# Decoding float32 weights with three VectorE operations in place of five

## The chip, the cores and the metric

The kernel runs on one core of a Trainium2 chip. The metric is the device time of one execution in microseconds (us); lower is better. A core has five engines that work side by side, each on its own queue in order: TensorE (PE, matrix products and transposes; its weight loads are shown as PEld), VectorE (DVE), ScalarE (ACT), GpSimd (POOL) and SyncE (SP, which issues transfers here).

## The reference

Three stages on 2304 tokens (4 batches of 576), all float32: an attention with 8 heads of 64, of which four heads see a band of 32 positions and four see every 32nd position; a gated feed-forward with an RMS norm; a second gated feed-forward without a norm.

```python
def _moe_ref(x, w_gate, w_val, w_out, rms_g):
    rms = np.sqrt(np.mean(x * x, axis=-1, keepdims=True) + 1e-06)
    xn = x / rms * rms_g
    g = xn @ w_gate                       # 512 -> 1536
    silu = g * (1.0 / (1.0 + np.exp(-g)))
    val = xn @ w_val
    return (silu * val @ w_out).astype(np.float32)

def reference(**kwargs):
    attn_out = _attn_ref(q, k, v)         # (4, 8, 576, 64), masked softmax(q k^T / 8) v
    x = np.ascontiguousarray(attn_out.transpose(0, 2, 1, 3)).reshape(B * S, H * D)
    x = _moe_ref(x=x, **moe_kwargs)
    return _moe2_ref(x=x, **moe2_kwargs)  # the same without rms and rms_g
```

The weights and the second layer's weights reach the kernel as 64-bit floats, two 32-bit words each, which it reads as integers.

## The kernel before

**The products.** Every float32 operand of a feed-forward product is kept as two halves, a high part `hi` that TensorE takes exactly and a low part `lo`, the rest. A product is then three matmuls: hi with hi, hi with lo, lo with hi (`proj`, `down`). The high part is made by a ScalarE copy that rounds, the low part by a VectorE subtraction (`split_x` for tokens, `hidden` for the hidden layer).

**The weights** come in 72 tiles of 128 x 512: for layer m, chunk c (12 of them) and z = 0, 1, 2 (gate, value, out). `weight_step` makes one tile in phases: `load` (a transfer of 512 KB of 64-bit words into `raw`, three buffers), two empty phases, `scale`, `bits`, `hi`. In `scale` ScalarE reads the high words as if they were floats and scales them (`dh`, L173), and converts the low words to an integer (`dr`, L174). In `bits` VectorE puts a float32 together by integer operations:

- L184 shifts `dh` and masks it, L186 adds the sign out of `raw`: the result is `df`, the weight cut to its upper bits;
- L188 keeps the exponent of `df`, L189 puts the low words' bits into `dr`, L191 multiplies the two: that is the low half, written to the weight tile `w` directly.

In `hi` ScalarE copies `df` into the tile's high half (L195). `dh` and `dr` have two buffers each.

**The order.** The program is written as products of chunks with `point()` calls between their pieces. At each point, every started step (attention pieces, weight tiles) runs its next phase, and new steps are started at a set pace; a scheduler then puts each engine's instructions in an order by priorities (weight tiles have the lowest). Weight work is placed behind the last attention or feed-forward instruction of its engine (`behind`).

**The stages.** First only attention of batch 0 runs (strided heads, local heads, RMS norm: `ss` holds the sums of squares, `mean`, `dg` and L595 apply the norm), together with the first weight tiles; then the products of the first layer begin on the first 256 tokens (`xh`, `xl` are the halves of the tokens, `b_g` and `b_v` the PSUM banks of gate and value), with the attention of later batches between them. 18 weight tiles (chunks 0 to 5 of layer 1) are decoded in this beginning; the first layer uses them for nearly all tokens before chunks 6 to 11 are decoded from 344 us on, and the other 54 tiles follow beside long products.

Of the kernel before, what the change touches and what calls it, by code (L numbers as in the profile page):

```python
# [8 lines left out]
F32 = mybir.dt.float32  # L9
F32R = mybir.dt.float32r  # L10
U32 = mybir.dt.uint32
AF = mybir.ActivationFunctionType
ALU = mybir.AluOpType
# [8 lines left out]
PRIO_W = -150  # L22
# [3 lines left out]
def attn_ffn_ffn(ctx: ExitStack, tc: tile.TileContext, q, k, v, w1g, w1v, w1o, rms_g, w2g, w2v, w2o, out):  # L26
    nc = tc.nc
# [15 lines left out]
    dec = ctx.enter_context(tc.tile_pool(name="dec", bufs=2))  # L43
# [88 lines left out]

    LOW = 2.0 ** -9 * (1 - 2.0 ** -23)
    WSRC = {1: (w1g, w1v, w1o), 2: (w2g, w2v, w2o)}
    wt = {}
    wdone = set()
# [6 lines left out]
    def free(m, c):  # L145

        i = order.index((m, c))
        return slot_of[m, c] in wpool and (i < RING or order[i - RING] in wused) and (m == 1 or state["rest"])
# [4 lines left out]
    def weight_step(m, c, z):  # L153
        cell = {}

        def load():
            w = WSRC[m][z].bitcast(U32)
            if z == 2:
                src = w[c * 128:(c + 1) * 128, :].rearrange("p (k f) -> p k f", k=KC)
            else:  # L160
                src = w[:, c * 256:(c + 1) * 256].rearrange("(k p) f -> p k f", p=128)
            r = dec.tile([128, KC, 256], U32, tag="raw", name="raw", bufs=3)
            (nc.sync if att else nc.sync).dma_start(out=r, in_=src)
            words = r.rearrange("p k f -> p (k f)").rearrange("p (n s) -> p n s", s=2)
            cell["lw"], cell["hw"] = words[:, :, 0], words[:, :, 1]

        def scale():

            h = dec.tile([128, 512], F32, tag="dh", name="dh")
            r = dec.tile([128, 512], U32, tag="dr", name="dr")  # L170
            cell["h"], cell["r"] = h, r
            with behind("act"):
                nc.scalar.activation(out=h, in_=cell["hw"].bitcast(F32), func=AF.Copy, scale=2.0 ** -112)  # L173
                nc.scalar.activation(out=r, in_=cell["lw"], func=AF.Copy, scale=LOW)  # L174

        def bits():


            h, r = cell["h"].bitcast(U32), cell["r"]
            s = slot_of[m, c]  # L180
            cell["t"] = t = wpool[s].tile([128, 2, KC * 128], F32R, tag=f"w{s}_{z}", name=f"w{m}_{c}_{z}")
            cell["f"] = f = dec.tile([128, 512], F32, tag="df", name="df")
            with behind("dve"):
                nc.vector.tensor_scalar(out=h, in0=h, scalar1=3, scalar2=0x7FFFF000, op0=ALU.logical_shift_left,  # L184
                                        op1=ALU.bitwise_and)
                nc.vector.scalar_tensor_tensor(out=f.bitcast(U32), in0=cell["hw"], scalar=0x80000000, in1=h,  # L186
                                               op0=ALU.bitwise_and, op1=ALU.bitwise_or)
                nc.vector.tensor_scalar(out=h, in0=f.bitcast(U32), scalar1=0xFF800000, scalar2=None, op0=ALU.bitwise_and)  # L188
                nc.vector.scalar_tensor_tensor(out=r, in0=cell["hw"], scalar=23, in1=r,  # L189
                                               op0=ALU.logical_shift_left, op1=ALU.bitwise_or)  # L190
                nc.vector.scalar_tensor_tensor(out=t[:, 1], in0=r, scalar=2.0 ** -43, in1=cell["h"], op0=ALU.mult, op1=ALU.mult)  # L191

        def hi():
            with behind("act"):
                nc.scalar.copy(out=cell["t"][:, 0], in_=cell["f"])  # L195
            wt[m, c, z] = cell["t"]
            wdone.add((m, c, z))

        return Step([load] + [wait] * 2 + [scale, bits, hi], lambda: free(m, c), PRIO_W)

    def behind(eng):

        return tc.issue_after(last[eng]) if eng in last else nullcontext()
# [501 lines left out]
    def gate(m, c, n, xs):  # L705
        need_w(m, c, 0)
        gv = GV[0]
        GV.append(GV.pop(0))
        pg = bank(gv[0])
        proj(pg, n, wt[m, c, 0], xs)  # L710
        hp, w = pools["h"]
        s = hp.tile([128, w], F32, tag="s", name="sg")
        silu(s, pg, n)
        point()
        need_w(m, c, 1)
        pv = bank(gv[1])
        proj(pv, n, wt[m, c, 1], xs)
        hh = hp.tile([128, w], F32R, tag="hh", name="hh", bufs=3)
        hl = hp.tile([128, w], F32R, tag="hl", name="hl", bufs=3)
        hidden(s, pv, hh, hl, n)  # L720
        point()
        return hh, hl
# [79 lines left out]
    att.load(0, 1)  # L802
    att.load_v(0, 1)
    wq += [weight_step(m, c, z) for m, c in order for z in range(3)]
    for _ in range(0):
        start(wq.pop(0))
# [31 lines left out]
    for si, (m, t0, n, c0, c1) in enumerate(segs):  # L838
# [17 lines left out]
        for c in range(c0, c1):  # L856
            h = gate(m, c, n, xs)
# [60 lines left out]
```

## Time and profile before

| | us |
|---|---|
| runs | 1076.64, 1082.42, 1082.6 |
| median of the runs | 1082.42 |
| profiled execution | 1075.61 |
| its span, first to last instruction | 1073.7 |
| PE busy | 1039.3 (97%) |
| PEld busy | 914.4 (85%) |
| DVE busy | 510.8 (48%) |
| ACT busy | 442.8 (41%) |
| POOL busy | 58.7 (5%) |

The mean granted clock of TensorE is 0.969 of its full speed. Busy shares are means over the whole span. In the page's 40 slices of 27 us each, PE shows 4, 8, 7, 8 tenths in the first four slices and 9 in nearly all others, and DVE 3, 8, 9, 8 tenths in the first four, so that the beginning has to be read apart from the rest.

### The profile page before, as it was taken

To read this page: it belongs to the slowest core of one execution; us is meant where nothing else is said; L and a number is where in the kernel's file an instruction comes from. 1 tells how busy PE (TensorE), PEld (TensorE's weight loads), DVE (VectorE), ACT (ScalarE), POOL (GpSimd) and SP (SyncE) were. 2 spreads that over 40 slices of the span, in tenths; PEclk is the share of its full clock that TensorE was granted. 3 is DMA by queue.
4 is the path that set the end of the run, shared out by engine and by line. 5 is a ranking of instruction groups with operands and counts; after the bars stand their busy time and mean duration, and the time that the engine had idled before them with its cause. 6 is when DMAs were issued, how large, how long until landed. Compare 5 with 4: busy or idle time off the path is not lost.

```text
span 1073.7 us, 15937 instructions
## 1 busy us (share of the span) xinstructions
PE 1039.3 (97%) x6056; PEld 914.4 (85%) x6056; DVE 510.8 (48%) x1296; ACT 442.8 (41%) x1082; POOL 58.7 (5%) x83
## 2 busy tenths in 40 slices
PE   4878999999999999999999999999999999999998
PEld 3668999999999999998888898888888888888887
DVE  3898536445445883692222589312224512222212
ACT  5977546636634662561211467222123312212111
POOL 3212102102100000000000000000000000000000
PEclk9657999999999999999999999999999999999999
DMA  7685233233014551372021366111111102030202
GB/s 194 169 215 172 77 103 94 88 98 94 25 60 133 172 160 58 113 234 89 20 79 62 118 206 213 37 62 40 40 40 65 34 1 94 14 98 1 78 1 89
DMA packets 104260, 100.39 MB, mean 94 GB/s; under 512 B 40564, under 2 KB 92476, under 8 KB 103544
## 3 DMA queue, kind: packets, MB, share of 16 engines
q1 hardware_dynamic: 103992, 99.10, 30.2%
q8 instruction: 48, 0.79, 0.3%
q0 software_dynamic: 192, 0.28, 0.1%
q14 instruction: 28, 0.23, 0.1%
HBM read 77.47 MB, written 21.89 MB: 93 GB/s over the span
## 4 chain that ended last, share of the span: by engine, by line
PE 91%; DVE 4%; DMA 3%; ACT 1%; issue 0%; SPq 0%; DVEq 0%; ACTq 0%
PE b_y L63 28%; PE b_a L63 28%; PE b_v L63 16%; PE b_g L63 16%; PE b_a L66 2%; DMA raw<-in_moe_w_gate_dram 1%; DVE dr L189 1%; DVE df L186 1%; DVE w L191 1%; DMA kn<-in_k_dram 1%; ACT e L409 0%; DMA part<-ob 0%; DMA xf<-x_d 0%; SPq L266 0%; DVE xl L692 0%
## 5 line engine op out<-in xcount | busy, mean ns | idle before, releaser
L63 PE MATMUL b_a<-xh,w 128*128 128x512 f32 (+3 forms) x816 | 232.8, 361 | 0.0
L63 PE MATMUL b_g<-xh,w 128*128 128x512 f32 (+3 forms) x696 | 192.8, 342 | 2.0 <-DVE sg L668 2.0
L63 PE MATMUL b_v<-xh,w 128*128 128x512 f32 (+3 forms) x696 | 193.1, 342 | 0.0
L63 PE MATMUL b_y<-hh,w 128*128 128x320 f32 (+3 forms) x624 | 165.3, 329 | 1.7 <-DVE ob L75 1.7
L63 PEld LDWEIGHTS b_a<-xh,w 128*128 128x128 f32 x816 | 148.6, 190 | 21.5
L678 ACT CAST hh<-sg 128x512 fp32r<-128x512 f32 (+3 forms) x138 | 72.6, 526 | 199.4 <-DVE sg L677 175.9
L63 PE MATMUL b_a<-xl,w 128*128 128x512 f32 (+3 forms) x408 | 147.3, 361 | 0.0
L63 PEld LDWEIGHTS b_g<-xh,w 128*128 128x128 f32 x696 | 125.5, 191 | 15.1 <-DVE sg L668 2.3
L63 PEld LDWEIGHTS b_v<-xh,w 128*128 128x128 f32 x696 | 125.3, 191 | 12.9 <-issue 0.9
L63 PE MATMUL b_y<-w,hh 128*128 128x512 f32 x432 | 133.3, 390 | 0.0
L63 PEld LDWEIGHTS b_y<-hh,w 128*128 128x128 f32 x624 | 110.0, 188 | 9.9 <-DVE ob L75 1.9
L63 PE MATMUL b_g<-xl,w 128*128 128x512 f32 (+3 forms) x348 | 117.0, 336 | 0.0
L63 PE MATMUL b_v<-xl,w 128*128 128x512 f32 (+3 forms) x348 | 116.8, 336 | 0.0
L677 DVE TENSOR_TENSOR sg<-sg,b_v 128x512 f32<-128x512 f32 (+3 forms) x51 | 31.2, 612 | 164.5 <-PE b_v L63 160.9
L677 DVE TENSOR_TENSOR sg<-sg,b_a 128x512 f32<-128x512 f32 (+3 forms) x51 | 31.2, 611 | 153.3 <-PE b_a L63 152.8
L679 DVE TENSOR_TENSOR hl<-sg,hh 128x512 fp32r<-128x512 f32 (+3 forms) x138 | 80.9, 586 | 43.1 <-ACT hh L678 42.6
L63 PE MATMUL b_y<-hl,w 128*128 128x320 f32 (+3 forms) x312 | 100.9, 323 | 0.0
L63 PEld LDWEIGHTS b_y<-w,hh 128*128 128x128 f32 x432 | 80.4, 188 | 16.2
L63 PEld LDWEIGHTS b_a<-xl,w 128*128 128x128 f32 x408 | 77.6, 190 | 10.9
L670 ACT ACTIVATE sg<-b_a 128x512 f32<-128x512 f32 (+3 forms) x51 | 27.4, 538 | 139.3 <-PE b_a L63 139.1
L63 PE MATMUL b_y<-w,hl 128*128 128x512 f32 x216 | 84.0, 389 | 0.0
L670 ACT ACTIVATE sg<-b_g 128x512 f32<-128x512 f32 (+3 forms) x51 | 27.4, 538 | 123.2 <-PE b_g L63 123.0
(126 smaller groups left out, 1356.8 us busy)
## 6 DMA issues: line engine op xcount, KB each, us to landing
raw<-in_moe_w_gate_dram SPq DMA_DIRECT2D x24, 512.0 KB
raw<-in_moe_w_val_dram SPq DMA_DIRECT2D x24, 512.0 KB
raw<-in_moe_w_out_dram SPq DMA_DIRECT2D x24, 512.0 KB
xf<-y_d SPq DMA_DIRECT2D x5, 1024.0 KB
out_dram<-ob SPq DMA_DIRECT2D x18, 256.0 KB
xf<-x_d SPq DMA_DIRECT2D x8, 512.0 KB
part<-ob SPq DMA_DIRECT2D x14, 256.0 KB
ob<-part SPq DMA_DIRECT2D x14, 256.0 KB
```

The source lines that it names most:

```text
L63: traced(nc.tensor.matmul(out_, a, b_, start=start, stop=stop))
L66: traced(nc.tensor.transpose(out_, a, one))
L186: nc.vector.scalar_tensor_tensor(out=f.bitcast(U32), in0=cell["hw"], scalar=0x80000000, in1=h, op0=ALU.bitwise_and, op1=ALU.bitwise_or)
L189: nc.vector.scalar_tensor_tensor(out=r, in0=cell["hw"], scalar=23, in1=r, op0=ALU.logical_shift_left, op1=ALU.bitwise_or)
L191: nc.vector.scalar_tensor_tensor(out=t[:, 1], in0=r, scalar=2.0 ** -43, in1=cell["h"], op0=ALU.mult, op1=ALU.mult)
L670: last["act"] = ins_of(nc.scalar.activation(out=s[:, :n], in_=pg[:, :n], func=AF.Silu))
L677: nc.vector.tensor_tensor(out=s[:, :n], in0=s[:, :n], in1=pv[:, :n], op=ALU.mult)
L678: last["act"] = ins_of(nc.scalar.copy(out=hh[:, :n], in_=s[:, :n]))
L679: last["dve"] = ins_of(nc.vector.tensor_tensor(out=hl[:, :n], in0=s[:, :n], in1=hh[:, :n].bitcast(F32), op=ALU.subtract))
```

## The change

A tile now takes two bit operations and a subtraction on VectorE. ScalarE's two conversions stay; the constant of the second is another, so that the integer `dr` already holds the float's low bits in place. L180 (new numbering) puts the sign out of `raw` into `dr`, L181 shifts `dh` and adds `dr`: `dh` is now the whole float32. ScalarE copies it into the high half (L187), and VectorE subtracts that half from `dh` into the low half (L192) in a phase of its own, `lo`. `df` is gone; `dh` lives until the subtraction. A weight step has seven phases in place of six.

```diff
-    LOW = 2.0 ** -9 * (1 - 2.0 ** -23)
+    LOW = 2.0 ** -29 * 0.9365
...
         def bits():
             h, r = cell["h"].bitcast(U32), cell["r"]
+            with behind("dve"):
+                nc.vector.scalar_tensor_tensor(out=r, in0=cell["hw"], scalar=0x80000000, in1=r, op0=ALU.bitwise_and, op1=ALU.bitwise_or)
+                nc.vector.scalar_tensor_tensor(out=h, in0=h, scalar=3, in1=r, op0=ALU.logical_shift_left, op1=ALU.bitwise_or)
+
+        def hi():
             s = slot_of[m, c]
             cell["t"] = t = wpool[s].tile([128, 2, KC * 128], F32R, tag=f"w{s}_{z}", name=f"w{m}_{c}_{z}")
-            cell["f"] = f = dec.tile([128, 512], F32, tag="df", name="df")
+            with behind("act"):
+                nc.scalar.copy(out=t[:, 0], in_=cell["h"])
+
+        def lo():
+            t = cell["t"]
             with behind("dve"):
-                nc.vector.tensor_scalar(out=h, in0=h, scalar1=3, scalar2=0x7FFFF000, op0=ALU.logical_shift_left,
-                                        op1=ALU.bitwise_and)
-                nc.vector.scalar_tensor_tensor(out=f.bitcast(U32), in0=cell["hw"], scalar=0x80000000, in1=h,
-                                               op0=ALU.bitwise_and, op1=ALU.bitwise_or)
-                nc.vector.tensor_scalar(out=h, in0=f.bitcast(U32), scalar1=0xFF800000, scalar2=None, op0=ALU.bitwise_and)
-                nc.vector.scalar_tensor_tensor(out=r, in0=cell["hw"], scalar=23, in1=r,
-                                               op0=ALU.logical_shift_left, op1=ALU.bitwise_or)
-                nc.vector.scalar_tensor_tensor(out=t[:, 1], in0=r, scalar=2.0 ** -43, in1=cell["h"], op0=ALU.mult, op1=ALU.mult)
-
-        def hi():
-            with behind("act"):
-                nc.scalar.copy(out=cell["t"][:, 0], in_=cell["f"])
-            wt[m, c, z] = cell["t"]
+                nc.vector.tensor_tensor(out=t[:, 1], in0=cell["h"], in1=t[:, 0].bitcast(F32), op=ALU.subtract)
+            wt[m, c, z] = t
             wdone.add((m, c, z))
 
-        return Step([load] + [wait] * 2 + [scale, bits, hi], lambda: free(m, c), PRIO_W)
+        return Step([load] + [wait] * 2 + [scale, bits, hi, lo], lambda: free(m, c), PRIO_W)
```

The change also moves instructions. **First place:** VectorE before the norm of batch 0's first tokens, from `mean` to the products with `gcol`. Before (the numbered names are buffers; `raw`, `dh`, `dr`, `df` belong to weight tiles 1_2_2 and 1_3_0):

```order
L576 TENSOR_SCALAR mean_874<-b_y3_860 128x2
L184 TENSOR_SCALAR dh_485<-dh_485 128x512
L188 TENSOR_SCALAR dh_454<-df_471 128x512
L186 SCALAR_TENSOR_TENSOR df_499<-raw_439,dh_485 128x512
L189 SCALAR_TENSOR_TENSOR dr_486<-raw_439,dr_486 128x512
L584 TENSOR_SCALAR dg_885<-ident_87,rstd_877 128x128 x2
L556 TENSOR_TENSOR ss_780<-ss_780,sq_899 128x320
L191 SCALAR_TENSOR_TENSOR w1_2_2_470<-dr_455,dh_454 128x512
L188 TENSOR_SCALAR dh_485<-df_499 128x512
L556 TENSOR_TENSOR ss_780<-ss_780,sq_902 128x320
L595 SCALAR_TENSOR_TENSOR x00_815<-x00_815,gcol_92,b_g_905 128x256 x2
```

The same place now:

```order
L573 TENSOR_SCALAR mean_820<-b_y3_806 128x2
L181 SCALAR_TENSOR_TENSOR dh_427<-dh_427,dr_428 128x512
L553 TENSOR_TENSOR ss_726<-ss_726,sq_845 128x320
L581 TENSOR_SCALAR dg_831<-ident_87,rstd_823 128x128 x2
L553 TENSOR_TENSOR ss_726<-ss_726,sq_848 128x320
L181 SCALAR_TENSOR_TENSOR dh_457<-dh_457,dr_458 128x512
L192 TENSOR_TENSOR w1_2_2_455<-dh_427,w1_2_2_455 128x512
L592 SCALAR_TENSOR_TENSOR x00_761<-x00_761,gcol_92,b_g_851 128x256 x2
```

Between `mean` and `dg` stand one decode operation and a sum in place of four decode operations, and nothing stands between `dg` and the second sum `ss`. Behind the products with `gcol`, three decode operations and one subtraction for the tokens (L692) stood ahead of the next `mean`; now one decode operation does.

**Second place:** VectorE at the second `b_g` bank of the first layer's products, from the maximum of a softmax piece (`sums`) to the product that frees the bank (L668, now L665). Before, with `raw`, `dh`, `dr`, `df` of tiles 1_4_1 and 1_4_2:

```order
L419 TENSOR_SCALAR sums_1076<-sums_1076 126x4
L186 SCALAR_TENSOR_TENSOR df_626<-raw_556,dh_610 128x512
L184 TENSOR_SCALAR dh_632<-dh_632 128x512
L189 SCALAR_TENSOR_TENSOR dr_633<-raw_581,dr_633 128x512
L420 RECIPROCAL rc_1094<-sums_1076 126x4
L188 TENSOR_SCALAR dh_610<-df_626 128x512
L419 TENSOR_SCALAR sums_1098<-sums_1098 108x4
L186 SCALAR_TENSOR_TENSOR df_652<-raw_581,dh_632 128x512
L679 TENSOR_TENSOR hl_1072<-sg_1023,hh_1071 128x256
L400 ISA e_1175,nb_1176<-b_a0_1161,ms_91 108x108
...
L668 SCALAR_TENSOR_TENSOR sg_1114<-sg_1114,b_g_1087 128x256
```

Now:

```order
L416 TENSOR_SCALAR sums_1022<-sums_1022 126x4
L180 SCALAR_TENSOR_TENSOR dr_611<-raw_560,dr_611 128x512
L181 SCALAR_TENSOR_TENSOR dh_588<-dh_588,dr_589 128x512
L417 RECIPROCAL rc_1040<-sums_1022 126x4
L416 TENSOR_SCALAR sums_1044<-sums_1044 108x4
L665 SCALAR_TENSOR_TENSOR sg_1060<-sg_1060,b_g_1033 128x256
```

The product that frees the bank stands behind two decode operations in place of five, and ahead of the softmax piece and of `hl`. The order of TensorE is the same in both kernels from the norm of batch 0 on, but for the names of buffers, and so are the numbers of its instructions and the order of GpSimd.

## Rows read from the trace of the kernel before

**Rows 1.** Busy time by stretch: length, then busy (count) per engine, clock, DMA.
```profile
17.10:71.00 53.90, 39.14 (x252) 30.29 (x251) 48.77 (x165) 49.16 (x156) 13.25 (x14) 0.64 0.84 205
71.00:91.40 20.40, 20.40 (x105) 18.12 (x103) 16.98 (x68) 14.11 (x48) 3.67 (x3) 0.62 0.73 214
91.40:108.70 17.30, 13.79 (x90) 12.33 (x89) 17.11 (x42) 13.56 (x34) 5.95 (x5) 0.80 0.34 110
108.70:344.00 235.30, 234.88 (x1971) 222.66 (x1972) 115.85 (x453) 124.62 (x411) 30.41 (x38) 1.00 0.29 87
344.00:1073.00 729.00, 724.09 (x3593) 624.55 (x3591) 311.29 (x566) 236.82 (x428) 0.00 (x0) 1.00 0.25 82
```

**Rows 2.** VectorE's lines by form, 0 to 115 us: busy, mean ns, idle before.
```profile
L186 DVE SCALAR_TENSOR_TENSOR df<-raw,dh 128x512 uint32<-128x512 uint32 x18 | 14.2, 790 | 0.1
L189 DVE SCALAR_TENSOR_TENSOR dr<-raw,dr 128x512 uint32<-128x512 uint32 x18 | 14.0, 779 | 0.0
L191 DVE SCALAR_TENSOR_TENSOR w<-dr,dh 128x512 fp32r<-128x512 uint32 x18 | 13.3, 741 | 0.1
L184 DVE TENSOR_SCALAR dh<-dh 128x512 uint32<-128x512 uint32 x18 | 8.0, 443 | 1.8 <-ACT dh L173 1.7
L188 DVE TENSOR_SCALAR dh<-df 128x512 uint32<-128x512 uint32 x18 | 7.5, 414 | 0.1
```

**Rows 3.** VectorE's timeline: start, length, instruction, idle before.
```profile
56.12 0.41 DVE L184 TENSOR_SCALAR dh<-dh 128x512 uint32<-128x512 uint32 x1
56.45 0.68 DVE L189 SCALAR_TENSOR_TENSOR dr<-raw,dr 128x512 uint32<-128x512 uint32 x1
57.05 0.68 DVE L186 SCALAR_TENSOR_TENSOR df<-raw,dh 128x512 uint32<-128x512 uint32 x1
...
62.34 0.43 DVE L184 TENSOR_SCALAR dh<-dh 128x512 uint32<-128x512 uint32 x1 [1.40 <-ACT dh L173]
```

**Rows 4.** VectorE's lines by form, whole span: a subtraction of halves.
```profile
L692 DVE TENSOR_TENSOR xl<-xf,xh 128x512 fp32r<-128x512 f32 x40 | 26.5, 686 | 29.4 <-ACT xh L691 29.4
```

**Rows 5.** The chain of waits, 53 to 62 us: start, length, what.
```profile
53.60 0.91 DVE dr L189
54.54 7.02 DMA raw<-in_moe_w_gate_dram
...
61.65 0.67 ACT dh L173
```

**Rows 6.** TensorE's timeline: matmuls that waited, and the first product at 74.04.
```profile
64.56 1.22 PE L63 MATMUL b_g<-dg,ones 128*128 128x128 f32 x4 [2.53 <-DVE dg L584]
...
70.49 0.90 PE L66 MATMUL b_a<-ident,qn 108*64 108x108 f32 x4 [1.71 <-DVE mean L576]
...
74.04 0.58 PE L63 MATMUL b_g<-xh,w 128*128 128x256 f32 x1
...
92.80 0.39 PE L63 MATMUL b_g<-xh,w 128*128 128x256 f32 x1 [1.39 <-DVE sg L668]
...
94.71 1.10 PE L66 MATMUL b_a<-ident,e 126*126 126x126 f32 x4 [0.67 <-POOL e L426]
...
103.56 0.39 PE L63 MATMUL b_g<-xh,w 128*128 128x256 f32 x1 [0.57 <-DVE sg L668]
...
108.67 0.34 PE L66 MATMUL b_a<-ident,qn 64*128 64x64 f32 x2 [0.53 <-DVE qT L75]
```

**Rows 7.** TensorE's timeline: pairs of equal matmuls, early and late.
```profile
84.53 0.63 PE L63 MATMUL b_v<-xh,w 128*128 128x256 f32 x2
...
87.97 0.40 PE L63 MATMUL b_g<-xh,w 128*128 128x256 f32 x2
```

**Rows 8.** GpSimd's timeline around 91 us.
```profile
91.47 2.02 POOL L313 MEMSET qT<- 128x2304 f32 x1 [7.72 <-PE b_a L63]
93.45 2.06 POOL L426 TENSOR_TENSOR e<-e,rc 126x504 f32<-126x504 f32 x2
```

**Rows 9.** Waits of ScalarE, 0 to 115 us: us in total, times, longest.
```profile
ACT w L195 <- DVE df L186: 3.8, 4, 2.0
```

## The prediction

> **What bounds the kernel now.** I read the busy time by stretch first. From 108.7 us to the end TensorE is busy in 959.0 of 964.3 us at clock 1.00, while VectorE is busy in 427 of them [rows 1]. There a shorter decode gives nothing: the 54 tiles of that part lie beside full TensorE work, and its order there is unchanged. All that the change can gain or lose lies ahead of 108.7 us. In that part VectorE is the fullest engine: 48.8 of 53.9 us from 17.1 to 71, then 17.0 of 20.4, then 17.1 of 17.3 [rows 1]. But it isn't alone. ScalarE is busy in 49.2 of the first 53.9 us, and TensorE without a break from 71 to 91.4, at a mean clock of 0.62 [rows 1].
>
> TensorE's waits come next: 2.53 us for `dg`, 1.71 us for `mean`, the first product of the layer at 74.04, then 1.39, 0.67, 0.57 and 0.53 us at 92.8, 94.7, 103.6 and 108.7; all but the 0.67, which is GpSimd's, are put down to VectorE [rows 6]. The third view is the chain of waits: L189 ends at 54.5, only then the transfer of the raw words of tile 1_3_0 starts, takes 7.02 us, and ScalarE begins with it at 61.65 [rows 5]. VectorE in turn stands idle for 1.40 us until ScalarE is through, at 62.34 [rows 3].
>
> **What is removed and added.** 18 tiles are decoded in the beginning. Their five operations cost 14.2, 14.0, 13.3, 8.0 and 7.5, together 57.0 us of duration, 3.17 us a tile [rows 2]. Removed in kind are one three-operand operation and both two-operand ones; a subtraction of 128 x 512 halves takes 0.686 us [rows 4] and stands for the third three-operand one. By durations the tile then costs 0.79 + 0.78 + 0.69 = 2.26, a gain of 0.91 us.
>
> The timeline says less: a two-operand operation starts at 56.12, its successor of three operands at 56.45 and the next at 57.05 [rows 3], so what one takes from VectorE's queue is 0.33 and 0.60 us, not 0.41 and 0.68. By starts a tile is 3 x 0.60 + 2 x 0.33 = 2.46 before and 1.80 now: 0.66 us, 18 x 0.66 = 11.9 us in all. I take the starts, and keep 18 x 0.91 = 16.4 us as the upper end, since durations include the times an operation was held up. The Trainium skill ("VectorE: DVE Perf Modes", "The DRAIN you can't avoid") says that the next operation does not start until the pipe is empty; by that the durations would add up and the gain would be 16.4 us, and the 0.08 us of overlap in this trace speaks against it.
>
> ScalarE's three conversions of a tile stay, and their number too. The transfers stay; a raw buffer comes free earlier, because its last reader on VectorE is now the first of the tile's operations (L180) and no longer L186 or L189, behind others.
>
> **What of it lies on the path, step by step.**
>
> *To the first product (17.1 to 74.0).* Ten tiles, 6.6 us of VectorE's queue by starts. ScalarE's free time of 53.9 - 49.2 = 4.7 us [rows 1] bounds what the part up to 60 us can give, so I count 2.5 us there, about half of it. From 60.8 on I follow the new order. Before, `dg` started at about 64.2, since four decode operations stood ahead of it and the first of them waited for ScalarE until 62.34 [rows 3]. Now one decode operation and a sum stand there, and the raw words of tile 1_3_0, the late transfer, come earlier: its buffer is released by ScalarE's reading of tile 1_2_0 and no longer by L189. `dg` then goes about 1.4 us earlier, bound by ScalarE's squares instead. The second sum follows it at once, without the two operations (0.60 + 0.33) that stood between. `mean` of the next part, which costs TensorE 1.71 us [rows 6], has one decode operation ahead of it where three and a token subtraction stood: another 1.2. That is 3.5 us, with 2.5 a gain of 6 us at 74.04. Bounds: 0 if ScalarE alone sets the pace, 9.1 (ten times 0.91) if VectorE alone does.
>
> *From the first product to 91.4.* TensorE has no idle time here, so nothing of VectorE's is on the path. But the same pair of matmuls takes 0.63 us at 84.5 and 0.40 at 88.0 [rows 7]: the granted clock goes from its lower level, 1.2 GHz, to 2.4 GHz near 86.5, after TensorE had worked without a break since 70.5. If the waits of 2.53 and 1.71 us go, that unbroken work begins at about 63 to 66 in place of 70.5, and the higher level comes earlier against the program: I take 2 us, from 4 us less work at the lower level. Bounds: 0 and 6 (the 12.4 us from 74.0 to 86.4 all at the higher level).
>
> *From 91.4 to 108.7.* The wait of 1.39 us at 92.80 is for the product that frees a `b_g` bank; with three decode operations fewer ahead of it, and the softmax piece and `hl` behind it, it goes. What is late next is GpSimd: the transposes at 94.71 need a multiplication that stands behind a clearing of 2.02 us, which itself waits for TensorE [rows 8]. TensorE then arrives 1.4 us earlier and waits longer for the same end. I count nothing for the first two waits, and 1.5 us for the last ones (0.57 and 0.53, and a shorter one between). Bounds: 0 and 5.5 (all waits, and the clock's second low stretch in part).
>
> The sum is 6 + 2 + 1.5 = 9.5 us: 1075.6 - 9.5 = 1066.1 against the profiled execution. The median of the runs shown lies 6.8 above that execution, the lowest run 1.0 above it; the runs stand at two levels, 1076 and 1082.5. With the same two levels the change gives 1066 to 1073, and I name 1069.
>
> **The rivals.**
>
> *The cover is elsewhere (0.25).* ScalarE, 91% busy up to 71 us, and GpSimd's clearing at 91.5 set the pace, and VectorE's shorter queue only gives it more idle time. For it: ScalarE waits for `df` in just 4 cases, 3.8 us in all [rows 9]. Against it: the 2.53 and 1.71 us, which are VectorE's. Then the gain is 0 to 4 us: 1072 to 1082.
>
> *VectorE waits for the rounding copy (0.10).* So far the two engines passed a tile on once, and the rounding copy was the last step, with nothing of VectorE's behind it. Now the subtraction sits in VectorE's queue behind a ScalarE copy that itself stands behind up to seven exponentials, and softmax maxima, sums and `dg` stand behind the subtraction; and ScalarE's next `dh` needs the buffer that the subtraction frees. The Trainium skill ("TensorE: Matmul & The Clock Gate", on engine queue depths) calls both queues strictly first in, first out; the new rows of the order agree that nothing passes the subtraction. Price: the subtractions stand in nine pairs; a tile's longest wait between the two engines was 2.0 us [rows 9]. One such wait for a pair is 18 us, less 11.9 gained: 6 us slower, 1082; one for each tile is 36 - 11.9 = 24 us slower, 1100. It decides from 0.66 us of waiting per tile on. Against it: the subtractions were placed well behind their copies in the new order, mostly a point or more later, and TensorE's queue still hides part.
>
> *Everything pays (0.15).* VectorE's shortening reaches the path in full, 11.9 to 16.4 us, or the clock stays at the higher level for more of the beginning: 1059 to 1064.
>
> That the change doesn't do what it says, fewer operations on VectorE, I can exclude: the new order has the three operations for every tile.
>
> **How the numbers follow.** The forecast has 0.50, the others 0.25, 0.10 and 0.15. The range takes in the forecast's own bounds as far as the full case (1059, and 1 us for the runs) and the covered case up to a little above the median of before: 1058 to 1084. About 1% of the median, 10.8 us, is what a measurement can tell from no change, so faster means below 1071.6. The forecast's 9.5 us straddles that: I give half of its 0.50 to faster, half to the same. With the 0.15 and 0.02 from the covered case, faster has 0.42; same has 0.25 + 0.23 + 0.03 = 0.51; slower, from the waiting subtraction alone, 0.07.
>
> **What would show it.** In the new profile the first product `b_g<-xh,w` should start at 67 to 69 us (before: 74.04); VectorE's busy time up to that point should be some 8 us less and ScalarE's the same; TensorE's wait for `dg` should be under 1.2 us and that for `mean` under 0.6; the transfer of tile 1_3_0 should start before 52 us; TensorE should wait for GpSimd, not for `sg`, near the transposes of the second batch's probabilities; from the point where TensorE is full on, some 965 us should remain, as before. I am wrong if the first product starts later than 72, if VectorE shows idle time ended by ScalarE's copies (L187) of more than 5 us in the beginning, or if the time after that point differs by more than 3 us.

## The result and the profile after

The changed kernel took 1066.95 us (median of 4 runs, 1065.9 to 1067.59) beside 1081.62 for the kernel before (4 runs, 1076.64 to 1082.6): ratio 0.9873, 95% interval 0.984 to 0.9905. Measured again beside the experiments (7 runs and 15) it was 1067.03 against 1076.58: ratio 0.9915, interval 0.9884 to 0.9946. The second is the better estimate, since the kernel before varies more than its first runs showed: over four later sessions and 74 runs it lies between 1071.4 and 1083.4, with session medians of 1075.9 to 1076.6. So the change gives some 9 us (0.0085 x 1076.6). The profiled pair differs by 8.2 us: 1067.38 (span 1065.6) against 1075.61 (span 1073.7).

The stretches of the changed kernel that answer to [rows 1], cut at the same places of TensorE's order (columns as there):

```profile
17.10:64.73 47.63, 38.31 (x250) 30.14 (x247) 39.78 (x137) 45.74 (x151) 14.23 (x14) 0.62 0.91 215
64.73:87.25 22.52, 21.11 (x106) 18.34 (x103) 17.23 (x65) 17.12 (x56) 1.79 (x3) 0.60 0.91 262
87.25:103.01 15.76, 12.18 (x90) 11.12 (x89) 15.01 (x35) 12.27 (x34) 6.35 (x5) 0.89 0.34 109
103.01:338.92 235.91, 234.87 (x1972) 222.64 (x1972) 114.65 (x449) 124.62 (x411) 30.54 (x38) 1.00 0.28 84
338.92:1065.00 726.08, 722.42 (x3593) 623.10 (x3591) 276.04 (x458) 233.71 (x428) 0.00 (x0) 1.00 0.25 82
```

In the first stretch VectorE (third pair) falls from 48.77 to 39.78 us, and ScalarE (fourth) less, to 45.74 of 47.63 us: it is 96% busy where it was 91%. The first stretch is 6.3 us shorter, the third 1.5, the last 2.9; the second and fourth are 2.1 and 0.6 longer. In the second stretch, where TensorE had no idle time, it now has 22.52 - 21.11 = 1.41 us. In the third its idle time has not changed, 17.30 - 13.79 = 3.51 before and 15.76 - 12.18 = 3.58 now; its granted clock has, from 0.80 to 0.89.

VectorE's decode, by line, 0 to 110 us, against [rows 2]:

```profile
L180 DVE SCALAR_TENSOR_TENSOR dr<-raw,dr 128x512 uint32<-128x512 uint32 x18 | 16.2, 898 | 0.6 <-ACT dr L174 0.6
L192 DVE TENSOR_TENSOR w<-dh,w 128x512 fp32r<-128x512 f32 x18 | 13.4, 749 | 0.7 <-ACT w L187 0.6
L181 DVE SCALAR_TENSOR_TENSOR dh<-dh,dr 128x512 uint32<-128x512 uint32 x18 | 12.9, 721 | 1.7 <-ACT dh L173 1.6
```

They make 42.5 us where the five made 57.0, 14.5 less. Behind the second bar stands the idle time ahead of each line and what ended it: 0.6 us by ScalarE's rounding copy L187, in all.

TensorE's timeline, where it waited, against [rows 6]:

```profile
60.03 1.22 PE L63 MATMUL b_g<-dg,ones 128*128 128x128 f32 x4 [1.23 <-DVE dg L581]
64.21 0.90 PE L66 MATMUL b_a<-ident,qn 108*64 108x108 f32 x4 [1.11 <-DVE mean L573]
65.87 0.93 PE L66 MATMUL b_a<-ident,kn 108*64 108x108 f32 x4 [0.76 <-ACT kT L73]
67.45 2.07 PE L63 MATMUL b_a<-kT,qT 64*126 64x126 f32 x8 [0.65 <-ACT qT L73]
69.45 0.58 PE L63 MATMUL b_g<-xh,w 128*128 128x256 f32 x1
...
81.22 0.63 PE L63 MATMUL b_g<-xh,w 128*128 128x256 f32 x2
...
83.81 0.40 PE L63 MATMUL b_g<-xh,w 128*128 128x256 f32 x2
...
90.38 1.10 PE L66 MATMUL b_a<-ident,e 126*126 126x126 f32 x4 [2.21 <-POOL e L423]
...
98.16 0.39 PE L63 MATMUL b_g<-xh,w 128*128 128x256 f32 x1 [0.68 <-DVE sg L665]
...
99.82 0.66 PE L66 MATMUL b_a<-ident,qn 128*128 128x128 f32 x4 [0.68 <-DVE qT L75]
```

Set against before, place by place: the first product is 4.6 us earlier (69.45 for 74.04), the transposes of `e` 4.3 (90.38 for 94.71), the product at 103.56 5.4 (98.16), the transposes at 108.67 5.7, and the end 8.1 by the spans. The waits for `dg` and `mean` are 1.9 us shorter together, but behind `mean` two waits for ScalarE's copies of `kT` and `qT` have appeared, 1.41 us. A pair of equal products still falls from 0.63 to 0.40 us near the same place in the program, between 81.22 and 83.81 us here and between 85.81 and 87.97 before.

GpSimd, at the wait of 2.21 us (against [rows 8]):

```profile
87.32 2.02 POOL L310 MEMSET qT<- 128x2304 f32 x1 [8.34 <-PE b_a L63]
89.30 3.20 POOL L423 TENSOR_TENSOR e<-e,rc 126x504 f32<-126x504 f32 x3
```

Behind 108.7 us the gain grows from 5.7 to 8.1 us, and that comes from a place that the prediction did not look at. In the kernel before, TensorE waits near 355 us, and the chain of waits there runs through a store (first TensorE's timeline, then the chain: start, length, what):

```profile
354.62 0.39 PE L63 MATMUL b_y<-hh,w 128*128 128x256 f32 x1 [1.72 <-DVE ob L75]
```

```profile
348.47 0.43 ACT ob L73
...
348.92 5.03 DMA part<-ob
...
354.07 0.50 DVE ob L75
...
354.62 0.39 PE b_y L63
```

`finish` copies four banks of partial outputs into `ob`, which has two buffers. The third copy needs the first store to have left its buffer. SyncE's and VectorE's timelines show when that store goes and when the copy can, before and after:

```profile
346.85 0.38 SPq L163 DMA_DIRECT2D raw<-in_moe_w_gate_dram  x1
348.43 0.38 SPq L163 DMA_DIRECT2D raw<-in_moe_w_val_dram  x1
348.92 1.14 SPq L766 DMA_DIRECT2D part<-ob  x2
```

```profile
341.49 0.38 SPq L163 DMA_DIRECT2D raw<-in_moe_w_gate_dram  x1
342.09 0.38 SPq L163 DMA_DIRECT2D raw<-in_moe_w_val_dram  x1
344.02 0.81 SPq L763 DMA_DIRECT2D part<-ob  x2
```

```profile
347.07 0.49 DVE L75 COPY ob<-b_y 128x320 f32<-128x320 f32 x1 [0.33 <-DMA part<-ob]
```

Before, the second of two transfers of 512 KB was issued 0.49 us ahead of the store, and the store took 5.03 us; TensorE stood idle for 1.72 us, in its wait for the copy (L75). Now that transfer goes 1.93 us ahead, the copy starts 3.05 us after the store's issue, and TensorE does not wait. And in the kernel before the wait has an echo, in the stretch from 356 us on (columns as [rows 1]):

```profile
354.60:356.00 1.40, 1.38 (x11) 1.39 (x12) 1.40 (x4) 1.10 (x3) 0.00 (x0) 1.00 0.63 247
356.00:359.60 3.60, 3.60 (x20) 3.60 (x19) 2.73 (x6) 2.51 (x5) 0.00 (x0) 0.53 0.62 207
359.60:362.00 2.40, 2.40 (x22) 2.40 (x22) 1.92 (x5) 1.16 (x3) 0.00 (x0) 1.00 0.02 8
```

TensorE is busy throughout, but for 3.6 us at a granted clock of 0.53, which does 0.47 x 3.6 = 1.7 us less work than the full clock. In the changed kernel the clock is 1.00 from 343 to 357 us. So the wait cost 1.72 us and then up to 1.7 more. Against the program, the lead of the changed kernel grows from 5.1 us at 344 to 7.0 behind the wait and 8.5 behind the stretch at the low clock; the last stretch as a whole is 2.9 us shorter. The fourth lost 0.6 to two waits of 0.5 us, for `dg` and `x` of a later batch, where one of 0.3 us for `dg` stood.

### The profile page after: what moved, and what is told of

Read it like the earlier page. It is cut to its first block, busy times and chain, and to the rows that moved or that the text cites. A ratio compares the mean times of both kernels' runs of the same rounds, so it can differ in the third digit from the quotient of the medians.

```text
span 1065.6 us, 15758 instructions
## 1 busy us (share of the span) xinstructions
PE 1036.2 (97%) x6056; PEld 912.0 (86%) x6056; DVE 463.8 (44%) x1152; ACT 438.2 (41%) x1082; POOL 58.4 (5%) x83
## 4 chain that ended last, share of the span: by engine, by line
PE 91%; DMA 3%; ACT 3%; DVE 2%; SPq 1%; issue 1%; DVEq 0%; ACTq 0%
PE b_y L63 28%; PE b_a L63 27%; PE b_v L63 17%; PE b_g L63 16%; PE b_a L66 2%; DMA xf<-x_d 1%; SPq L263 1%; DMA raw<-in_moe_w_val_dram 1%; DMA raw<-in_moe_w_gate_dram 1%; ACT e L406 1%; ACT dh L173 0%; DMA raw<-in_moe_w_out_dram 0%; ACT x L73 0%; DVE x L592 0%; DVE dr L180 0%
```

## The experiments

Eleven kernels beside the change, in four sessions, each with the kernel before on the same chip. All ratios are to the kernel before. "First product" is the start of the first `b_g<-xh,w` in the profiled execution, "to the end" the span less that.

| kernel | ratio, 95% interval | median, us | first product | to the end |
|---|---|---|---|---|
| before, profiled for the prediction | | | 74.04 | 999.7 |
| x_before | 1.0003, 0.9978 to 1.0029 | 1076.91 | 78.23 | 996.8 |
| x_front | 0.9955, 0.9928 to 0.9982 | 1070.26 | 68.86 | 994.9 |
| x_rest | 0.9971, 0.9942 to 1.0 | 1073.21 | 77.23 | 1000.1 |
| x_plus2 | 1.0014, 0.9985 to 1.0043 | 1079.34 | 73.40 | 1003.2 |
| change, first measurement | 0.9873, 0.984 to 0.9905 | 1066.95 | 69.45 | 996.2 |
| y_after | 0.9915, 0.9884 to 0.9946 | 1067.03 | 70.54 | 995.7 |
| y_lonow | 0.9916, 0.9885 to 0.9947 | 1067.9 | 69.79 | 992.7 |
| y_noconv | 0.9906, 0.9878 to 0.9935 | 1065.4 | 67.65 | 996.1 |
| y_qd | 0.99, 0.987 to 0.993 | 1065.4 | 67.34 | 994.3 |
| z_raw4 | 0.9907, 0.9883 to 0.9931 | 1065.41 | 69.73 | 994.0 |
| z_eng6 | 0.9894, 0.9872 to 0.9917 | 1063.32 | 70.20 | 990.8 |
| z_qdeng6 | 0.9907, 0.9881 to 0.9933 | 1065.09 | 72.92 | 994.5 |
| w_ob3 | 1.0012, 0.9985 to 1.0039 | 1077.72 | 73.46 | 1000.9 |

**The kernel before, once more (x_before).** No edit.

> The kernel before, unchanged, profiled once more, since its runs stand at two levels (1076.6, and 1080.8 to 1082.6) and the profile so far is of the lower one. Theory: the upper level is lost ahead of 110 us, where TensorE's clock is at its lower level for different lengths; the first product then starts at 74 as before and TensorE is full later, at 112 to 115 us in place of 108.7. Rival: it is lost later, in one wait of TensorE beside the long products (2 to 6 us after 340 us). If the lower level is profiled again: span 1073 to 1075, and nothing is learned.

Same time, but another course: the first product came 4.2 us later than in the first profile, the rest was 2.9 us shorter. Most of the loss ahead of the first product lies in TensorE's clock. In the first profile it was at its higher level from 38.7 to 49.0 us; here it stayed at the lower one from 21.2 until 51.9. The first row is of the first profile, the second of x_before (columns as [rows 1]):

```profile
38.70:48.90 10.20, 8.06 (x62) 5.78 (x61) 9.15 (x39) 8.71 (x37) 2.48 (x3) 1.00 0.43 121
38.70:48.90 10.20, 9.47 (x46) 7.23 (x45) 5.84 (x27) 5.14 (x24) 1.65 (x2) 0.50 0.49 143
```

At the lower clock TensorE is the fullest engine there, and VectorE and ScalarE stand idle for almost half of the time. So single profiles of one kernel differ by some 4 us at a given place, and a step of the prediction has to be judged from more than one, and from executions with a like course of the clock.

**The change in parts (x_front, x_rest).** The three operations for the 18 tiles of the beginning alone, and for the other 54 alone; the other tiles keep the five of before.

```diff
+        new = m == 1 and c < HC              # x_front; x_rest: not (...)
...
+                nc.scalar.activation(out=r, in_=cell["lw"], func=AF.Copy, scale=LOW if new else LOW5)
...
+        tail = [bits, hi, lo] if new else [bits5, hi5]
```

> The three operations only for the 18 tiles of the beginning (layer 1, chunks 0 to 5), the five operations for the other 54. Theory (the beginning pays): first product at 69 to 70 us, TensorE full from 103 us on, time 1067 to 1070; only the 1.7 us at the `ob` copy near 350 us can come back. Rival (VectorE's work as a whole pays): 18 of 72 tiles bring a quarter of the 14.7 us between the medians, time 1076 to 1079.

> The reverse: five operations for the first 18 tiles, three for the other 54. Theory (the beginning pays): first product at 74, time 0 to 3 us below the kernel before. Rival (VectorE's work as a whole pays): 54 of 72 tiles bring three quarters of it, 11 us below the kernel before.

The beginning gives about 4.8 us of median (0.9955), with the first product at 68.86; the rest about 3.1 (0.9971), with the first product as late as before, but its interval reaches 1.0, so that this part may be nothing. Together 0.9926, inside the interval of the whole. The beginning is the larger part, as the theory had it; whether it is all isn't settled by the times. The profile of x_front still has the wait at the copy of partial outputs, near 345 us, as the kernel before does:

```profile
344.72 0.39 PE L63 MATMUL b_y<-hh,w 128*128 128x256 f32 x1 [2.37 <-DVE ob L75]
```

There too the clock falls behind it, to 0.59 from 346 to 350 us. In x_rest TensorE is busy in all 726 us from 344 to 1070, and that wait is gone; its gain of 3.1 us is about what the wait and its echo cost, which is an argument and not a test.

That x_rest starts the products at 77.23 comes in the main from the clock of the beginning too. The view of granted clocks says 1.00 for it ahead of 51.6 us, but its matmuls there have the lengths of the lower level. The same pair, in the kernel before and in x_rest:

```profile
42.15 0.46 PE L63 MATMUL b_y<-kT,qT 128*128 128x96 f32 x2
```

```profile
45.94 0.74 PE L63 MATMUL b_y<-kT,qT 128*128 128x96 f32 x2
```

A product that starts at 47.20 in the first profile of before starts at 52.13 in x_before and at 51.73 in x_rest, 4.9 and 4.5 us later: more than the 4.2 and 3.2 that they lack at the first product. In w_ob3 it starts at 47.35, and in the changed kernel at 43.69.

**Two operations put back (x_plus2).** The new kernel with two two-operand operations more for each tile that change nothing.

```diff
+                for _ in range(2):
+                    nc.vector.tensor_scalar(out=r, in0=r, scalar1=0, scalar2=None, op0=ALU.bitwise_or)
```

> The changed kernel with two two-operand operations more for each tile (each an OR of `dr` with 0, in place, ahead of the other operations): five operations again, but with the new kernel's dependences. 18 x 2 x 0.33 = 12 us more of VectorE's queue in the beginning. Theory (the number of operations pays): about what the change gained is lost again, first product at 72 to 75 us, time 4 to 9 us above the changed kernel. Rival (the other order, the earlier free raw buffer and the shorter chain pay, not the number): first product at 69 to 71, time within 2 us of the changed kernel.

All of the gain is gone: 1.0014, first product at 73.40, and its lowest run, 1073.9, is above the highest of y_after, 1071.4, in another session. So the other order of the operations and the buffer `df` that fell away are not what pays; VectorE's time is. (The raw buffer comes free later here too, as the added operations stand ahead of L180; z_raw4 below speaks against that as the cause.) Three of TensorE's longer waits up to 110 us are VectorE's again, beside 3.8 us for GpSimd's `e` in two (engine, line, releaser: us in total, times, longest):

```profile
PE b_y L63 <- DVE ss L555: 2.3, 1, 2.3
PE b_a L66 <- DVE mean L575: 1.4, 1, 1.4
PE b_g L63 <- DVE dg L583: 0.8, 1, 0.8
```

x_plus2 shows no wait at the copy of partial outputs either, and yet is no faster than before: 1003.2 us from the first product on. Part of that is TensorE's wait for GpSimd's `e` at 94.4 us, 2.39 where before has 0.67. More is lost at a wait that neither kernel has, for a weight tile itself, and at the lower clock behind it (TensorE's timeline, then the stretch with columns as [rows 1]):

```profile
123.68 0.39 PE L63 MATMUL b_v<-xh,w 128*128 128x256 f32 x1 [3.36 <-ACT w L189]
```

```profile
124.20:131.10 6.90, 5.96 (x30) 5.47 (x31) 4.75 (x17) 3.45 (x13) 1.09 (x1) 0.51 0.23 76
```

So the added operations do not simply bring the kernel before back, and its first product is no clean price either: TensorE was at its lower clock from 35.5 to 56.0 us, like x_before. What the run shows is that the time of the whole depends on VectorE's operations.

**The change itself (y_after).** No edit.

> The changed kernel itself, for a ratio from more runs. If the two parts timed alone (0.9955 for the 18 tiles of the beginning, 0.9971 for the other 54) add up, its ratio to the kernel before is 0.9926, some 8 us less. If the profiled pair tells it (1067.4 against 1075.6) it is the same 0.992; if the first runs' medians do, 0.987. Rival: the parts share a gain (both move the same clock rise), then the whole is no better than the front part, 0.9955. In its profile the first product should start at 68.9 to 69.5 us and the copy of partial outputs near 350 us should not be waited for.

0.9915, as the two parts together had it; first product 70.54, a little later than expected; and no wait at the partial outputs.

**The subtraction right behind the rounding copy (y_lonow).**

```diff
                 nc.scalar.copy(out=t[:, 0], in_=cell["h"])
-
-        def lo():
-            t = cell["t"]
             with behind("dve"):
                 nc.vector.tensor_tensor(out=t[:, 1], in0=cell["h"], in1=t[:, 0].bitcast(F32), op=ALU.subtract)
...
-        return Step([load] + [wait] * 2 + [scale, bits, hi, lo], lambda: free(m, c), PRIO_W)
+        return Step([load] + [wait] * 2 + [scale, bits, hi], lambda: free(m, c), PRIO_W)
```

> The changed kernel with the subtraction placed in the same phase as the rounding copy, right behind it and not a point later. The rival of the prediction, that VectorE waits for that copy, is tested where it should be strongest: one wait of 0.7 to 2 us per pair of tiles in the beginning would show as 5 us or more of VectorE's idle time ended by ScalarE's copy (L187) up to 110 us and cost 3 to 8 us (ratio to before 0.996 to 1.0). If VectorE's queue is long enough that the copy is done anyway: idle below 2 us, and the time within 1 us of the changed kernel.

The same time, 0.9916. VectorE's wait for the copy, up to 110 us, is still small:

```profile
DVE w L189 <- ACT w L187: 0.6, 2, 0.3
```

So the rival of the waiting subtraction falls even without the phase that keeps them apart: VectorE's queue is long enough. Its profile shows something else. The first product is only 0.75 us ahead of y_after's, but the transposes of `e` are 4.55 us ahead (86.64 for 91.19), as TensorE's clock rose earlier. First y_after, then y_lonow, from the first product on (columns as [rows 1]; the clock is the third number from the end):

```profile
70.50:78.00 7.50, 7.50 (x31) 6.67 (x31) 6.71 (x26) 4.77 (x15) 0.00 (x0) 0.50 0.95 205
78.00:82.00 4.00, 4.00 (x19) 3.58 (x19) 2.33 (x13) 3.71 (x14) 1.03 (x1) 0.50 0.92 281
```

```profile
69.80:74.00 4.20, 4.20 (x18) 3.86 (x18) 4.07 (x15) 3.35 (x11) 0.00 (x0) 0.50 1.14 200
74.00:78.00 4.00, 4.00 (x32) 3.50 (x31) 4.00 (x22) 1.75 (x4) 0.43 (x1) 1.00 0.76 228
```

In both kernels TensorE works without a break from some 2 us ahead of the first product; the second is at 2.4 GHz from 74 us on, the first still at 1.2 GHz at 82. That is worth 4.55 - 0.75 = 3.8 us.

**ScalarE without one of its conversions (y_noconv).** It leaves out L174 for the 18 first tiles and reads a tile of zeros in its place, so that those weights lack their low words.

```diff
+                if not (m == 1 and c < HC):
+                    nc.scalar.activation(out=r, in_=cell["lw"], func=AF.Copy, scale=LOW)
...
```

> The changed kernel, leaving out ScalarE's conversion of the low words for the 18 tiles of the beginning (a tile of zeros stands in its place, so those weights lack their low bits): about 18 x 0.6 us less on ScalarE, VectorE's work the same. Theory that ScalarE, full in 40 to 60 us, has become the bound up to the first product: the first product comes 3 to 6 us before 69.45, the waits behind mean and for the ScalarE copies of qT shrink, and the time falls by 3 to 6 us against the changed kernel (ratio to before about 0.988). Rival that transfers or VectorE are the bound there: first product within 1 us of 69.45 and the time within 1 us of the changed kernel (ratio 0.9926).

ScalarE was busy 44.7 us from 17.1 to 69, 4.4 less than in y_after; the first product came at 67.65, 1.8 to 2.9 earlier than in the changed kernel's two profiles, and the median was 1.6 us lower, with intervals that overlap. Neither expectation holds. That ScalarE bounds part of the beginning fits, but it isn't shown: y_qd, which takes nothing from ScalarE ahead of the first product, has it at 67.34. VectorE now waited for transfers (up to 110 us):

```profile
DVE dr L183 <- DMA raw<-in_moe_w_val_dram: 5.6, 1, 5.6
...
DVE dr L183 <- DMA raw<-in_moe_w_gate_dram: 2.0, 1, 2.0
```

**GpSimd without its clearing (y_qd).** The zeroed query tile has its own buffer, cleared once.

```diff
+                if w == 4 * S and b:
+                    self.qk[b, half, which] = self.qk[0, half, which]
+                    return self.qk[b, half, which]
...
```

> The changed kernel with the zeroed query tile of the local heads in a buffer of its own, cleared once, so that GpSimd's clearing of 2.02 us at 87.3 and the later ones are gone. Theory that GpSimd is what is late next behind the shorter VectorE: TensorE's wait of 2.21 us before the transposes of e at 90.4 goes, and the time falls by 1 to 3 us against the changed kernel (ratio to before 0.990 to 0.9915). Rival that another wait (sg, ScalarE's qT) takes its place: within 0.5 us of the changed kernel.

The wait for `e` is gone; one for VectorE's `sg` stands just ahead of it, where it was before the change ([rows 6], 92.80):

```profile
86.90 0.39 PE L63 MATMUL b_g<-xh,w 128*128 128x256 f32 x1 [1.20 <-DVE sg L668]
```

So of the 2.2 us some 1.0 is won there. The median is 1.6 us under y_after's, but the intervals overlap, and the first product came earlier too: not settled.

**A fourth raw buffer (z_raw4).** `bufs=3` for `raw` becomes `bufs=4`.

> The changed kernel with a fourth buffer for the raw words, in the 4 KB a partition that the change gave back. Leaving out ScalarE's conversion showed VectorE waiting 5.6 and 2.0 us for transfers. Theory that the transfers come late because a buffer is free late: the waits for raw words (3.3 and 1.6 us of ScalarE up to 110 us in the profile of the changed kernel) go, the first product comes 2 to 4 us earlier, and the time falls by 2 to 4 us against the changed kernel (ratio to before 0.988 to 0.990). Rival that the transfer engines themselves are full (busy 0.89 from 17 to 69 us): the transfers are issued earlier but land no earlier, first product and time within 1 us of the changed kernel (0.9915).

ScalarE's waits for raw words (up to 110 us) fall from 5.4 us in y_after to 2.6, yet the first product is where it was (69.73) and the time within 1.6 us. The transfers were not what the changed kernel waited for, although the reason given, full transfer engines, isn't shown: they are 0.86 busy from 17.1 to 69 us where y_after's are 0.89.

**More copies on VectorE (z_eng6, z_qdeng6).** `self.turn % 100` becomes `self.turn % 6`, so that every sixth copy out of attention's banks goes to VectorE and not every hundredth; z_qdeng6 has y_qd's own query tile as well.

> The changed kernel with one in 6 of the copies out of the banks of attention on VectorE in place of one in 100, so that some of the time that VectorE gained is given to ScalarE's work: about 8 to 10 copies of 0.3 to 0.5 us up to 70 us, 3 to 4 us off ScalarE and on VectorE. Theory that ScalarE is the cover there, as leaving out its conversion gave 1.8 to 2.9 us at the first product: first product 1 to 2 us earlier, time 1 to 2 us below the changed kernel (ratio to before 0.990). Rival that VectorE still is the bound: first product 1 to 3 us later, time the same or up to 3 us above.

> Both: the zeroed query tile in its own buffer, and one in 6 copies on VectorE. If the two gains are of different stretches (GpSimd's clearing at 87 us, ScalarE's copies ahead of 69 us) they add up: 2 to 4 us below the changed kernel, ratio to before 0.988 to 0.990. If the first product is what both moved, no more than the better of the two: 0.990.

z_eng6 has the lowest median, 1063.32, and 0.9894 beside the 0.9915 of y_after; but their intervals overlap, its first product isn't earlier (70.20), and its clock rose early in the profiled execution, as in y_lonow. That ScalarE's share should go to VectorE is not shown. Both together add nothing (0.9907); the first product came at 72.92, in an execution at the lower clock from 33.4 to 53.8 us.

**A third buffer for partial outputs, in the kernel before (w_ob3).** `bufs=pools.get("ob", 2)` becomes `bufs=3`.

> The kernel before with a third buffer for the partial outputs (ob) in the first layer. In the traces of before, TensorE waits once near 350 us (1.7 to 2.4 us) for the copy of a partial output, which itself waits until an earlier store has left its buffer; the changed kernel doesn't show that wait, and the part of the change behind the beginning, timed alone, gave 0.9971. Theory that this wait is what that part gained: it goes, the copy waits for no store, and the time falls by 1.7 to 2.4 us, ratio to before 0.998, with the first product where before has it (74 to 78 us). Rival that the wait is covered or another takes its place (the next banks, the raw words of the next chunk): the wait goes but TensorE stands idle elsewhere between 344 and 360 us, ratio 1.0.

The rival came true, at the next bank: the wait went from the third copy to the fourth, which now needs the first store's buffer, and the time is the same. Chain of waits:

```profile
348.47 5.87 DMA part<-ob
...
354.42 0.43 ACT ob L73
...
354.89 0.38 PE b_y L63
```

There are four banks, so three buffers only move the wait (2.09 us of TensorE here, with the same echo: clock 0.88 on average from 350 to 364 us). The run confirms what sets its end, the store's landing 5.9 us after its issue; it could not take the wait away, and so does not price it.

## Why the prediction was right, and where its steps were not

The forecast was 1069 us, worked out from 9.5 us less than the profiled execution; measured were 1067 and, in the profiled pair, 8.2 less. In that pair the steps measure 4.6 us to the first product (forecast 6), -0.4 from there to 91.4 (forecast 2), 1.5 to 108.7 (forecast 1.5), -0.6 to 344 and 3.0 to the end (forecast 0 for both). So the main step is right and was put somewhat too high, the clock's step failed, and a place that was not looked at made up for both: that the sum came out so near is in part luck.

**To the first product: 6 us forecast.** In the profiled pair it was 4.6. Four executions with the old beginning (before, x_before, x_rest, w_ob3) have it at 74.04, 78.23, 77.23 and 73.46; four with the new one (the change, y_after, y_lonow, x_front) at 69.45, 70.54, 69.79 and 68.86, mean 69.7. The means differ by 6.1 us, but x_before and x_rest are the two with the low clock until 51.9 and 51.6; against the other two, mean 73.75, it is 4.1. Whether the change itself makes that course of the clock rarer is open: z_qdeng6 and x_plus2 have it too. The mechanism is the one named, by x_front (the 18 tiles alone bring the first product to 68.86, and the time down) and x_plus2 (with the operations back the gain is gone). Place by place the lead was 1.9 us at the products with `ss` near 58.8 (forecast 2.5 up to 60), 4.5 at `dg` and 6.3 behind `mean`; then two waits for ScalarE's copies, which the forecast did not have, took 1.7 back. The transfer of tile 1_3_0 came as foreseen, at 51.53 in place of 54.54. The wait for `dg` is 1.23 (forecast: under 1.2), that for `mean` 1.11 and not under 0.6. VectorE's busy time up to the first product fell by 6.7 us (51.05 to 44.39) where some 8 were forecast. The changed kernel's busy time from 40 to 60 us (columns as [rows 1]):

```profile
40.00:50.00 10.00, 8.16 (x67) 5.42 (x65) 9.42 (x29) 9.68 (x35) 4.14 (x5) 0.77 0.71 210
50.00:60.00 10.00, 8.01 (x74) 6.18 (x72) 7.33 (x16) 10.00 (x26) 1.23 (x2) 0.50 0.76 210
```

ScalarE is busy 9.68 and 10.00 of each 10 us; VectorE is still 9.42 in the first ten, but 7.33 in the second. That speaks for ScalarE as the engine that is full next, as the rival of the covering engine said for the whole; it is argued from these rows, and no run settles it. VectorE's saving, 14.5 us of duration, reached the path by less than half.

**The price of a tile.** Taken by starts, 0.60 us for a three-operand operation. In the new kernel one starts at 344.52 and the next at 345.12, with 0.68 us of duration: the same. The gain by durations, 14.5, lies under the 16.4 of the upper end above all because L180 was held up in the beginning: 898 ns on average, against 0.68 us at 344.52.

**The clock: 2 us forecast, nothing in the profiled pair.** This step failed. It said that unbroken work which begins earlier brings the rise earlier against the program. TensorE did begin earlier, but at 67.45 in place of 70.49 and not at 63 to 66, as the waits for ScalarE's copies had come in; against the program that is later than before, and the rise stayed near its place. And it is not bound to any place: x_before has it some 8 us sooner after its first product than the first profile of the same kernel, y_lonow some 9 us sooner than y_after. What the step also left out is the clock ahead of the first product, which moved that product by some 4 us in the kernel before. The Trainium skill ("TensorE: Matmul & The Clock Gate", Part 1) calls the ramp variable from run to run of one kernel; the traces agree, x_before and the first profile of that kernel above all. Whether the change moves the rise on average is open.

**From 91.4 on: 1.5 us forecast, 1.5 measured, for another reason.** The wait of 1.39 us for `sg` went and GpSimd's grew to 2.21, much as worked out. But the last waits did not shrink by the 1.5 us: 0.57, 0.35 and 0.53 before became 0.68, 0.68 and none. The middle one of before, which [rows 6] leaves out, is

```profile
104.89 0.66 PE L66 MATMUL b_a<-ident,qn 128*128 128x128 f32 x4 [0.35 <-DVE qT L75]
```

Idle time is the same in all (3.51 and 3.58 us); what got shorter is the second stretch at the low clock. The number is luck.

**The long part: 0 forecast, 2.4 measured.** "Beside full TensorE work" held on the average and overlooked the one wait of 1.72 us in that part, since a share of 724 in 729 us hides it. With the low clock behind it, it stands for the 3.0 us of the profiled pair; the two waits for `dg` and `x` took 0.6 back. That it goes is seen in the change, y_after and x_rest, that it stays in x_front; in y_lonow 0.70 us of it are left. x_rest gains by about as much, within an interval that reaches zero. No run took the wait alone away. Why the first store stands farther behind the second transfer in the changed kernel, 1.93 for 0.49 us, was read from the two timelines only; no run set that distance by itself.

**The rivals.** The waiting subtraction: excluded, 0.6 us for all tiles of the beginning in the change and in y_lonow, where its price began at 0.66 for each tile. The cover elsewhere: behind `mean` TensorE waits for ScalarE and at 90.38 for GpSimd, but the gain of 9 us is far above the 0 to 4 of this rival. Everything pays: no, 9 us and not 11.9.

## What to carry to other kernels

Read a mean busy share for single waits before counting a long stretch at nothing: one wait of 1.7 us in 729, with the low clock behind it, was a third of the profiled gain. A shorter operation on a full engine pays until the next queue is full; here the next was probably ScalarE, at 96%, with less than half of the saving on the path. And where one kernel's executions differ by 4 us because TensorE's clock took another course, take several profiles of both kernels, and set those with a like course side by side, before a step of a few us is believed. Where the view gives a granted clock of 1.00, the lengths of equal matmuls tell whether it was so.

## What was not expected of the hardware

- The rise of TensorE's granted clock is not tied to the program: under unbroken work from the first product on, its equal pairs first took 0.40 us from 6 us (x_before) to 14 us (the first profile) after the first product, in the same kernel. Ahead of the first product it came back to its higher level at 38.7 us in the first profile and at 51.9 in x_before, whose first product is 4.2 us later. The run times of y_after lie between 1062.6 and 1071.4 us at mean clocks of 0.982 down to 0.972.
- A store of 160 KB issued 0.49 us behind a transfer of 512 KB, and 2.07 behind another, took 5.03 us to land; issued 1.93 and 2.53 us behind them, its buffer was free at most 3.05 us after the issue.
- TensorE's clock fell for 3.6 us behind a single wait of 1.72 us in the middle of full work (before, 356.0 to 359.6), and did not fall behind one of 2.4 us in x_before (1.00 from 352 to 366).
- VectorE's three-operand operation takes 0.68 us alone; L180 at 85.12 in y_qd took 1.40, beside a GpSimd multiplication that started at 84.80.
